# A new order of the units in the attention stage of a sparse-attention and two-layer feed-forward kernel

## The chip, the cores and the metric

The kernel runs on one NeuronCore of a Trainium2 chip. The metric is the device time of one execution in microseconds (us). The kernel before takes 877.76 us, the median of three runs (877.35 to 877.94).

## The reference

The input is an attention of 4 batches, 8 heads, 512 local and 32 global tokens, 64 numbers per head. A global token attends to all 544 tokens. A local token attends to the 32 global ones and to the local ones at most 32 positions away. The softmax takes the maximum off first and divides by the sum. What comes out, 2176 tokens of 512 numbers, goes through two feed-forward layers:

```
s_g   = scale * q_g @ k_all.T;   out_g = softmax(s_g) @ v_all
s_l   = scale * q_l @ [k_g, k_l].T, masked to |i - j| <= 32 among local keys
out_l = softmax(s_l) @ [v_g, v_l]
h = relu(x @ w1_in);  x = (h * h) @ w1_out                    # 512 -> 2048 -> 512
h = x @ w2_in;  g = P(h) / (Q(h) + 1e-6);  out = g @ w2_out   # P cubic, Q quadratic in |h|
```

All weights come as 64-bit floats. The first layer's and the second layer's weights are 16 chunks each of w_in and w_out, every one 128 x 512.

## The kernel before, in words

**Stages.** The attention stage is a loop over steps `p`. Step p = 0 to 15 belongs to one pair of heads (two heads of 64 numbers lie on the 128 partitions). Behind it lies the feed-forward stage, 2 layers x 5 tiles of tokens x 16 chunks, each chunk an `mm1` (12 matmuls into one PSUM bank) and an `mm2`. Steps 16 and 17 of the attention loop already do the first two `mm1` and their elementwise part (`ew1`).

**A unit.** A pair has two units (p, 0) and (p, 1), 256 query rows each. A unit goes through these pieces:
- S: `scores`, 8 matmuls in 64 x 64 tiles of the array (L311), into the banks `s_ps[0:2]` for unit 0 and `s_ps[2:4]` for unit 1.
- `maxima`: VectorE adds the mask and takes the row minimum of the scaled scores (L320), for each of two halves j; it also moves the scores out of PSUM. `exps`: ScalarE's exponentials with their row sums (L328).
- `sums`, `norm`: VectorE adds 1e-9 and takes the reciprocal (L332, L336), GpSimd multiplies (L339, four instructions).
- T: `transp`, five 128 x 128 transposes on TensorE into `tc_ps[0]` and `tc_ps[1]` (L357, L358). `transp_evac`: ScalarE copies the first bank out (L362), VectorE the second (L364).
- P·V: `pv`, global columns in full 128 x 128 matmuls (L382), windows in 128 x 64 tiles (L376), and for unit 1 a piece with the global queries (L396), into `pv_ps[u]`. `pv_local` and `pv_global`: VectorE copies the result into x (L403, L410, L412).
- `p_tiles` takes the buffers of the transposed probabilities; `g_copies`: GpSimd writes the global queries' probabilities into them (L350).

**The global queries.** For each group g of two pairs: G, `g_scores`, matmuls into `s_ps[0:2]` (L432; `pv_ps` for g = 0), with the maxima on VectorE (L435, L436); `g_scale` (L441); `g_exps` on ScalarE (L445, L446); `g_norm` on VectorE (L450, L451) and GpSimd (L452); Gt, `g_transp`, transposes back into `s_ps[0:2]` (L461, L462) and two ScalarE copies (L464, L465). G runs in odd steps, Gt in even ones.

**Weights.** Ten chunks of layer 1 are converted during the attention stage. `w_load` brings a chunk by DMA two steps ahead (L88), `w_scale` is ScalarE's first pass one step ahead (L94), `w_float` three VectorE passes (L106, L108, L113), `w_split` a VectorE cast (L124), `w_rest` a GpSimd subtraction (L132). `slots` says in which step a chunk is converted. `x_high` (ScalarE, L156) and `x_low` (VectorE, L161) split the first tile of x, a quarter a step, in steps 9 to 13.

**Order.** The program is inside `tc.manual_schedule()`: every engine executes its instructions in the order in which the text issues them. Waits between engines follow from the tiles that are written and read; a tile of a pool with `bufs` buffers waits until the one that lay there `bufs` allocations earlier has been read for the last time. In a step of the loop TensorE's order is now S (p, 0); T (p-1, 0); P·V (p-2, 1); G in odd steps; S (p, 1); Gt in even steps; T (p-1, 1); P·V (p-1, 0). In VectorE's queue the maxima of G stand where `g_scores` is called, and `g_scale` and `g_exps` stand ahead of the maxima and exponentials of unit (p, 1).

Of the kernel before, what the change touches and what calls it, by code (L numbers as in the profile page):

```python
# [17 lines left out]
ALU = mybir.AluOpType  # L18
# [35 lines left out]
def body(ctx, tc, qT, kW, v, w1i, w1o, w2i, w2o, coef, out):  # L54
# [209 lines left out]
    msk_p = att.enter_context(tc.tile_pool(name="msk", bufs=1))  # L264
    ident = msk_p.tile([128, 128], F32, name="ident")
    mask = msk_p.tile([128, NB, KW], F32, name="mask")
    v_p = att.enter_context(tc.tile_pool(name="v", bufs=2))
    sm_p = att.enter_context(tc.tile_pool(name="sm", bufs=4))
    pt_p = att.enter_context(tc.tile_pool(name="pt", bufs=3))
    pg_p = att.enter_context(tc.tile_pool(name="pg", bufs=2))  # L270
    st_p = att.enter_context(tc.tile_pool(name="st", bufs=4))

    ff_p = {}

# [40 lines left out]
    def maxima(p, u, j):  # L315
        s, nm = sm[p, u][:2]
        for i in range(2):
            b, k = 2 * u + i, 2 * j + i
            o = s[:, KW * i:KW * i + KW, j]
            dve.tensor_tensor_reduce(out=o, in0=s_ps[2 * u + j][:, KW * i:KW * i + KW], in1=mask[:, b],  # L320
                                     scale=-0.125, scalar=3.0e38, op0=ALU.add, op1=ALU.min,
                                     accum_out=nm[:, k:k + 1])
# [37 lines left out]
    def transp_evac(p, u):  # L360
        p1, p2 = pT[p, u]
        act.copy(bass.AP(tensor=p1.tensor, offset=p1.offset, ap=[p1.ap[0], [320, 2], [192, 2], [1, 128]]),  # L362
                 tc_ps[0].rearrange("p (a b c) -> p a b c", a=2, b=2))
        dve.tensor_copy(p2, tc_ps[1][:, 0:128])  # L364

    def pv(p, u):

        v = vt[p // 2]
        c = pgT[p // 2][1]
        p1, p2 = pT.pop((p, u))  # L370
        bank = pv_ps[u]

        def win(w, o0, o1, stop=False):
            for j in range(2):
                jj = 2 * (p % 2) + j
                pe.matmul(bank[64 * j:64 * j + 64, o0:o1], v[:, VW * w + 64 * jj:VW * w + 64 * jj + 64],  # L376
                          p1[:, j, o0 + (32 if o0 >= 128 else 0):o1 + (32 if o0 >= 128 else 0)],
                          start=False, stop=stop, skip_group_check=True)

        def glob(i):  # L380
            o = VG + 256 * (p % 2) + 128 * i
            pe.matmul(bank[:, 160 * i:160 * i + 128], v[:, o:o + 128], p2, start=i == 0, stop=False,  # L382
                      skip_group_check=True)


        glob(0)
        glob(1)
        win(4 * u, 64, 160)
        win(4 * u + 1, 0, 64)
        win(4 * u + 2, 128, 224)  # L390
        win(4 * u + 3, 224, 288, stop=u == 0)
        if u:
            for j in range(2):
                jj = 2 * (p % 2) + j
                o = VE + 64 * jj
                pe.matmul(bank[64 * j:64 * j + 64, 128:160], v[:, o:o + 64], c[:, 32 * jj:32 * jj + 32],  # L396
                          start=False, stop=True, skip_group_check=True)

    def pv_local(p, half):
        b, hp = divmod(p, 4)  # L400
# [17 lines left out]
    pg2 = [pg_p.tile([128, 128], F32, tag=f"pl{i}", name=f"pl{i}", bufs=1) for i in range(2)]  # L418

    def g_scores(g):  # L420
        c1, c2 = s_ps[:2] if g else pv_ps
        for c in (c1, c2):
            for i in range(2):
                p = 2 * g + i
                o = slice(64 * i, 64 * i + 64)
                if c is c1:
                    keys = kt[p][:, KE:KE + KW * NB].rearrange("p (a b) -> p a b", a=NB)[:, :, 0:128]
                else:
                    last = kt[p][:, KC - 64:KC]
                    keys = bass.AP(tensor=last.tensor, offset=last.offset - (KC - 64 - KE - 128),  # L430
                                   ap=[last.ap[0], [KC - 64 - KE - 128, 2], [1, 32]])
                pe.matmul(c[o] if c is c1 else c[o, 0:64], qt[p][:, SL:], keys, start=True, stop=True,  # L432
                          tile_position=(0, 64 * i))
        m = st_p.tile([128, 8], F32, tag="gm", name="gm")
        dve.tensor_reduce(m[:, 0:1], c1[:, 32:], axis=AX.X, op=ALU.max)  # L435
        dve.tensor_reduce(m[:, 1:2], c2[:, 0:64], axis=AX.X, op=ALU.max)  # L436
        pgs[g] = pg[g % 2], m, c1, c2

    def g_scale(g):
        s, m, c1, c2 = pgs[g]  # L440
        dve.tensor_scalar(m[:, 2:3], m[:, 0:1], m[:, 1:2], -0.125, op0=ALU.max, op1=ALU.mult)  # L441

    def g_exps(g):
# [25 lines left out]
    with tc.manual_schedule():  # L469
# [33 lines left out]

        early = [(0, 0, j) for j in range(N_IN0)] + [(0, 1, j) for j in range(N_OUT0)]
        slots = {}
        for p, c in zip([4, 6, 8, 10, 12, 14, 16, 16, 17, 17], early):
            slots.setdefault(p, []).append(c)

        for k in range(7):
            pe.matmul(pv_ps[0], warm[:, 0:128], warm, start=True, stop=True)  # L510
        for p in range(NP + 2):
            if p == NP:
                open_ff()
            if 1 <= p and p + 3 < NP:
                load_qk(p + 3)
            if p == 1:
                load_v(1)
            if p >= 4 and p % 2 == 0 and p // 2 < NP // 2:
                load_v(p // 2)
            for c in slots.get(p + 2, []):  # L520
                w_load(*c)
            cv = slots.get(p, [])
            cur, pre = p < NP, 1 <= p <= NP
            odd = p % 2 == 1 and p + 2 < NP
            g = (p + 1) // 2

            def step(*k):
                for c in cv:
                    w_float(*c, k)

            if cur:
                sm_tiles(p, 0)
                scores(p, 0)
                maxima(p, 0, 0)
                exps(p, 0, 0)
            else:
                mm1(p - NP)
            if 2 <= p:
                pv_local(p - 2, 0)
            if pre:  # L540
                sums(p - 1, 1)
            if cur:
                maxima(p, 0, 1)
            if pre:
                norm(p - 1, 1)
                p_tiles(p - 1, 0)
                p_tiles(p - 1, 1)
                if p > 1:
                    g_copies(p - 1, 0)
                    g_copies(p - 1, 1)  # L550
            step(0)
            if 2 <= p:
                pv_global(p - 2, 0)
            step(1)
            if pre:
                transp(p - 1, 0)
                transp_evac(p - 1, 0)
            step(2)
            if cur:
                exps(p, 0, 1)  # L560
            if 2 <= p:
                pv(p - 2, 1)
            if odd and p > 1:
                g_scores(g)
            if cur:
                sm_tiles(p, 1)
                if p == 0:
                    for k in range(4):
                        pe.matmul(pv_ps[0], warm[:, 0:128], warm, start=True, stop=True)
                scores(p, 1)  # L570
                if odd and p > 1:
                    g_scale(g)
                    g_exps(g)
                maxima(p, 1, 0)
                sums(p, 0)
                norm(p, 0)
                exps(p, 1, 0)
                maxima(p, 1, 1)
            if p == 1:
                g_transp(0)  # L580
                g_copies(0, 0)
                g_copies(0, 1)
                g_scores(g)
                g_scale(g)
                g_exps(g)
            if odd:
                g_norm(g)
            for c in cv:
                w_split(*c, dve)
                w_rest(*c)  # L590
            if p % 2 == 0 and 0 < p < NP:
                g_transp(g)
            if 2 <= p:
                pv_local(p - 2, 1)
                pv_global(p - 2, 1)
            if pre:
                transp(p - 1, 1)
                transp_evac(p - 1, 1)
            if cur:
                exps(p, 1, 1)  # L600
            if p == 0:
                for k in range(4):
                    pe.matmul(pv_ps[0], warm[:, 0:128], warm, start=True, stop=True)
                g_scores(0)
                g_scale(0)
                g_exps(0)
                g_norm(0)
            if pre:
                pv(p - 1, 0)
            for c in slots.get(p + 1, []):  # L610
                w_scale(*c)
            if 9 < p <= 9 + KD:
                x_low(0, p - 10)
            if 9 <= p < 9 + KD:
                x_high(0, p - 9)
            if p >= NP:
                ew1(p - NP)
        att.close()
        act.activation(nf[:, 0:4], cf[:, 0:4], AF.Copy, scale=-1.0)
# [24 lines left out]
        split = []  # L644
        made = []
        back = list(reversed(second))
        used = [1, -1]

        def load():

# [45 lines left out]

        load()
        magnitudes(2)
        for s in range(2, 2 * S1):
            t, j = divmod(s, KF)  # L700
            mm1(s)
            if j >= LAG:
# [99 lines left out]
```

## Time and profile before

| | us |
|---|---|
| median of three runs | 877.76 |
| the profiled execution | 878.36 |
| its span, first to last instruction | 876.6 |
| PE busy in the span | 866.3 |
| VectorE (DVE) busy | 614.2 |
| ScalarE (ACT) busy | 548.2 |
| GpSimd (POOL) busy | 249.7 |

The granted TensorE clock was 1.0 of full speed over the whole span. PE is TensorE's matmuls, whose ends are modelled: they overlap in the pipeline, so the time that one needs is the distance from its start to the next start, and a busy PE row hides short waits. DVE and ACT instructions overlap a little in the same way. A row "x4" stands for four merged instructions and gives the start of the first and the time that they cover. In the chain of waits each row is a stretch in which that instruction was what the end of the program waited for.

### The profile page before, as it was taken

What the parts mean: (1) busy time and instruction counts of PE and PEld (TensorE: products, weight loads), DVE (VectorE), ACT (ScalarE), POOL (GpSimd) and SP (SyncE); (2) the same over time, 40 slices, a digit from 0 to 9 for tenths busy, and PEclk for the clock granted to TensorE, in tenths of its full rate; (3) what the DMA queues carried; (4) which work ended last, traced back from release to release, by engine and by line L of the source; (5) the groups of instructions that cost most, each with busy time, mean ns of one, the idle gap of its engine ahead of it and who ended that gap; (6) DMA issues with size and microseconds to landing.
All of it is one profiled execution on the core that took longest, in us unless ns stands there. A gap on an engine that the chain in (4) does not pass through costs nothing.

```text
span 876.6 us, 14522 instructions
## 1 busy us (share of the span) xinstructions
PE 866.3 (99%) x5335; PEld 772.1 (88%) x5335; DVE 614.2 (70%) x1355; ACT 548.2 (63%) x1173; POOL 249.7 (28%) x326
## 2 busy tenths in 40 slices
PE   8999999999999999999999999999999999999998
PEld 4777788888888999999999978888888999999998
DVE  5788888855554576552422599769777987987986
ACT  6888857763332343432444588668666876886885
POOL 4787854420000000000156342212221221221221
PEclk9999999999999999999999999999999999999999
DMA  9787549101653176140034200010001001001001
GB/s 348 273 329 264 222 151 409 41 1 37 178 142 113 39 220 190 54 147 1 15 119 125 73 20 1 0 49 1 1 0 49 1 1 37 1 1 37 1 1 37
DMA packets 27574, 81.67 MB, mean 93 GB/s; under 512 B 3184, under 2 KB 4976, under 8 KB 26480
## 3 DMA queue, kind: packets, MB, share of 16 engines
q1 hardware_dynamic: 27504, 80.76, 27.0%
q8 instruction: 42, 0.69, 0.3%
q14 instruction: 28, 0.23, 0.1%
HBM read 67.90 MB, written 12.85 MB: 92 GB/s over the span
## 4 chain that ended last, share of the span: by engine, by line
PE 92%; DVE 3%; POOL 2%; ACT 1%; issue 1%; DMA 1%; SPq 0%; POOLq 0%; ACTq 0%
PE tc L188 21%; PE pv L188 21%; PE s L175 14%; PE s L177 14%; PE s L176 14%; POOL sm L339 2%; PE pv L376 2%; PE tc L357 2%; PE pv L382 1%; PE s L311 1%; DMA k<-in_kW_dram 1%; DVE sm L320 1%; PE s L432 1%; DVE tt L251 0%; ACT gs L445 0%
## 5 line engine op out<-in xcount | busy, mean ns | idle before, releaser
L175 PE MATMUL s<-xh,w 128*128 128x384 f32 (+1 forms) x640 | 229.7, 359 | 0.0
L177 PE MATMUL s<-xh,w 128*128 128x384 f32 (+1 forms) x640 | 228.4, 357 | 0.0
L176 PE MATMUL s<-xl,w 128*128 128x384 f32 (+1 forms) x640 | 228.3, 357 | 0.0
L260 POOL TENSOR_TENSOR gl<-tt,gh 128x384 fp32r<-128x384 f32 (+1 forms) x79 | 89.8, 1137 | 268.2 <-ACT gh L259 205.2
L188 PE MATMUL tc<-gh,w 128*128 128x384 f32 (+1 forms) x640 | 152.8, 360 | 0.8 <-ACT gh L259 0.8
L188 PE MATMUL pv<-gh,w 128*128 128x384 f32 (+1 forms) x640 | 152.5, 360 | 0.0
L217 ACT ACTIVATE a<-s 128x384 f32<-128x384 f32 (+1 forms) x80 | 42.5, 531 | 156.1 <-PE s L177 156.1
L177 PEld LDWEIGHTS s<-xh,w 128*128 128x128 f32 x640 | 120.1, 188 | 11.4
L176 PEld LDWEIGHTS s<-xl,w 128*128 128x128 f32 x640 | 120.2, 188 | 10.8
L175 PEld LDWEIGHTS s<-xh,w 128*128 128x128 f32 x640 | 120.1, 188 | 10.5
L188 PEld LDWEIGHTS tc<-gh,w 128*128 128x128 f32 x640 | 115.9, 188 | 12.5 <-ACT gh L259 1.7
L188 PEld LDWEIGHTS pv<-gh,w 128*128 128x128 f32 x640 | 115.9, 188 | 11.8
L132 POOL TENSOR_TENSOR w<-raw,w 128x512 fp32r<-128x512 f32 x32 | 42.5, 1346 | 278.8 <-ACT w L126 265.5
L223 DVE TENSOR_TENSOR b<-a 128x384 f32<-128x384 f32 (+1 forms) x64 | 38.4, 599 | 116.1 <-ACT a L217 116.1
L188 PE MATMUL pv<-gl,w 128*128 128x384 f32 (+1 forms) x320 | 89.4, 360 | 0.0
L188 PE MATMUL tc<-gl,w 128*128 128x384 f32 (+1 forms) x320 | 89.2, 359 | 0.0
L237 DVE SCALAR_TENSOR_TENSOR a<-a,nf,b 128x384 f32<-128x384 f32 (+1 forms) x80 | 53.4, 667 | 32.3 <-ACT b L235 32.2
L234 ACT ACTIVATE a<-s 128x384 f32<-128x384 f32 (+1 forms) x80 | 42.0, 525 | 52.9 <-PE s L177 52.9
L339 POOL TENSOR_SCALAR sm<-sm,rs 128x160 f32<-128x160 f32 x128 | 59.1, 486 | 27.7 <-DVE x L410 8.7
L250 DVE SCALAR_TENSOR_TENSOR a<-a,b 128x384 f32<-128x384 f32 (+1 forms) x80 | 49.0, 612 | 22.0 <-ACT b L245 22.0
L188 PEld LDWEIGHTS tc<-gl,w 128*128 128x128 f32 x320 | 58.7, 188 | 6.0
L188 PEld LDWEIGHTS pv<-gl,w 128*128 128x128 f32 x320 | 58.7, 188 | 5.8
(117 smaller groups left out, 1344.8 us busy)
## 6 DMA issues: line engine op xcount, KB each, us to landing
v<-in_v_dram SPq DMA_DIRECT2D x8, 1408.0 KB, 8.3
k<-in_kW_dram SPq DMA_DIRECT2D x15, 592.0 KB, 6.5
r<-in_w1i_dram SPq DMA_DIRECT2D x16, 512.0 KB, 9.6
r<-in_w1o_dram SPq DMA_DIRECT2D x16, 512.0 KB, 10.2
raw<-in_w2i_dram SPq DMA_DIRECT2D x16, 512.0 KB, 4.1
st<-cv SPq DMA_DIRECT2D x32, 256.0 KB, 4.3
raw<-in_w2o_dram SPq DMA_DIRECT2D x16, 512.0 KB, 4.0
raw<-st SPq DMA_DIRECT2D x32, 256.0 KB, 2.7
```

The source lines that it names most:

```text
L132: pool.tensor_tensor(w[:, 1], f, w[:, 0].bitcast(F32), op=ALU.subtract)
L175: pe.matmul(ph, wh, hi[:, kk, :n], start=(kk == 0), stop=False)
L176: pe.matmul(ph, wh, lo[:, kk, :n], start=False, stop=False)
L177: pe.matmul(ph, wl, hi[:, kk, :n], start=False, stop=(kk == KD - 1))
L188: pe.matmul(acc_bank[d][:, :n], w[:, half, 128 * d:128 * d + 128], src[:, :n], start=start, stop=stop)
L217: act.activation(a, ph, AF.Relu)
L223: dve.tensor_tensor(b, a, a, op=ALU.mult)
L234: act.activation(a, ph, AF.Square)
L237: dve.scalar_tensor_tensor(a, in0=a, scalar=nf[:, 5:6], in1=b, op0=ALU.mult, op1=ALU.add)
L250: dve.scalar_tensor_tensor(a, in0=a, scalar=EPS1, in1=b, op0=ALU.add, op1=ALU.mult)
L260: eng.tensor_tensor(gl, t, gh.bitcast(F32), op=ALU.subtract)
L339: pool.tensor_scalar(e, e, rs[:, k:k + 1], 1.0, op0=ALU.mult, op1=ALU.mult)
```

## The change

The loop gets one step more (16 to 18 beside the pairs), and the third `mm1` moves into it. In a step, TensorE's order becomes S (p, 0); T (p-1, 0); P·V of (p-3, 1) with the global columns first; G in odd steps; P·V of (p-2, 0) with the global columns last; Gt in even steps; T (p-2, 1); S (p, 1). A unit (p, 1) is therefore scored at the end of step p, has its maxima and exponentials at the start of step p+1, is transposed at the end of step p+2 and multiplied with V in step p+3. The maxima of G move from `g_scores` to `g_scale`, which together with `g_exps` stands behind the sums of unit (p, 0). G of the second group goes to the transposes' banks. The VectorE part of `transp_evac` becomes a function of its own. Buffers: v 3 instead of 2, sm 6 instead of 4, pt 5 instead of 3, st 6 instead of 4. The slots of the ten early chunks move from steps 4, 6, 8, 10, 12, 14, 16, 16, 17, 17 to 8, 10, 12, 14, 16, 16, 17, 17, 18, 18, and a chunk of a step up to 14 is converted in two parts: two `w_float` passes at the end of its step, the third, the cast and the subtraction at the end of the next. The diff's core:

```diff
-    v_p = att.enter_context(tc.tile_pool(name="v", bufs=2))
-    sm_p = att.enter_context(tc.tile_pool(name="sm", bufs=4))
-    pt_p = att.enter_context(tc.tile_pool(name="pt", bufs=3))
+    v_p = att.enter_context(tc.tile_pool(name="v", bufs=3))
+    sm_p = att.enter_context(tc.tile_pool(name="sm", bufs=6))
+    pt_p = att.enter_context(tc.tile_pool(name="pt", bufs=5))
...
-        dve.tensor_copy(p2, tc_ps[1][:, 0:128])
+
+    def transp_evac2(p, u):
+        dve.tensor_copy(pT[p, u][1], tc_ps[1][:, 0:128])
...
-        glob(0)
-        glob(1)
-        win(4 * u, 64, 160)
+        if u:
+            glob(0, start=True)
+            glob(1)
+        win(4 * u, 64, 160, start=not u)
         win(4 * u + 1, 0, 64)
         win(4 * u + 2, 128, 224)
-        win(4 * u + 3, 224, 288, stop=u == 0)
+        win(4 * u + 3, 224, 288)
...
+        else:
+            glob(0)
+            glob(1, stop=True)
...
-        c1, c2 = s_ps[:2] if g else pv_ps
+        c1, c2 = s_ps[:2] if g > 1 else tc_ps if g else pv_ps
...
-        for p, c in zip([4, 6, 8, 10, 12, 14, 16, 16, 17, 17], early):
+        for p, c in zip([8, 10, 12, 14, 16, 16, 17, 17, 18, 18], early):
...
-        for p in range(NP + 2):
+        for p in range(NP + 3):
...
+            a = (p - 1, 0) if pre else None
+            b = (p - 3, 1) if 3 <= p else None
+            c = (p - 2, 0) if 2 <= p <= NP + 1 else None
+            d = (p - 2, 1) if 2 <= p <= NP + 1 else None
+            odd, even = p % 2 == 1 and 1 < p < NP - 2, p % 2 == 0 and 0 < p < NP
...
             if cur:
                 sm_tiles(p, 0)
                 scores(p, 0)
+            elif p - NP < 3:
+                mm1(p - NP)
+            if pre and p > 2:
+                maxima(p - 1, 1, 0)
+                exps(p - 1, 1, 0)
+            if cur:
                 maxima(p, 0, 0)
                 exps(p, 0, 0)
+            for n in (a, d):
+                if n:
+                    p_tiles(*n)
+                    if p > 1:
+                        g_copies(*n)
+            if a:
+                transp(*a)
+                transp_evac(*a)
+            if cur:
+                maxima(p, 0, 1)
+                exps(p, 0, 1)
+            if pre and p > 2:
+                maxima(p - 1, 1, 1)
+                exps(p - 1, 1, 1)
+            if a:
+                transp_evac2(*a)
+            if b:
+                pv(*b)
+            if odd:
+                g_scores(g)
+            if c:
+                pv(*c)
+            if b:
+                pv_local(*b)
+                pv_global(*b)
+            if even:
+                g_transp(g)
+            if d:
+                transp(*d)
+            if cur:
+                sums(p, 0)
+                norm(p, 0)
+            if odd:
+                g_scale(g)
+                g_exps(g)
             if pre:
                 sums(p - 1, 1)
+                norm(p - 1, 1)
+            if c:
+                pv_local(*c)
+                pv_global(*c)
+            if d:
+                transp_evac(*d)
+                transp_evac2(*d)
+            if odd:
+                g_norm(g)
+            for w in first:
+                w_float(*w, (0, 1))
+            for w in second:
+                w_float(*w, (2,))
+            for w in whole:
+                w_float(*w)
+            for w in second + whole:
+                w_split(*w, dve)
+                w_rest(*w)
             if cur:
                 sm_tiles(p, 1)
...
                 scores(p, 1)
+            if p < 2:
+                for j in range(2):
+                    maxima(p, 1, j)
+                    exps(p, 1, j)
...
+            if p == 1:
+                g_transp(0)
+                g_copies(*a)
+                g_scores(1)
+                g_scale(1)
+                g_exps(1)
+                g_norm(1)
...
-        for s in range(2, 2 * S1):
+        for s in range(3, 2 * S1):
```

## Rows read from the trace of the kernel before

**Rows 1.** The page, the chain that ended last, share of the span by engine

```profile
PE 92%; DVE 3%; POOL 2%; ACT 1%; issue 1%; DMA 1%; SPq 0%; POOLq 0%; ACTq 0%
```

**Rows 2.** Windows: stretch, length, busy of PE, PEld, DVE, ACT, POOL, clock, DMA

```profile
24.95:57.64 32.69, 32.06 (x468) 25.43 (x465) 26.18 (x151) 27.28 (x107) 23.36 (x54) 1.00 0.72 265
57.64:110.89 53.25, 51.52 (x737) 40.94 (x733) 46.88 (x247) 47.04 (x178) 42.76 (x90) 1.00 0.68 262
...
80.56:94.13 13.57, 13.12 (x187) 10.32 (x185) 12.57 (x65) 12.13 (x46) 11.03 (x22) 1.00 0.57 219
```

**Rows 3.** The chain of waits in 54.06:67.22: start, us, what

```profile
54.06 0.94 PE s L432 x4
...
55.02 0.66 DVE gm L435
...
57.00 0.69 POOL sm L339 x2
```

**Rows 4.** Timeline of TensorE, one unit, and T behind Gt: start, us, instruction

```profile
64.41 0.77 PE L311 MATMUL s<-k,q 64*64 64x160 f32 x16
65.12 0.74 PE L357 MATMUL tc<-ident,sm 128*128 128x128 f32 x4
...
66.35 0.78 PE L376 MATMUL pv<-p,v 128*64 128x96 f32 x16
...
67.05 0.63 PE L432 MATMUL s<-k,q 128*64 128x512 f32 x2
...
23.11 0.64 PE L357 MATMUL tc<-ident,sm 128*128 128x128 f32 x4
...
24.23 0.78 PE L376 MATMUL pv<-p,v 128*64 128x96 f32 x16
```

**Rows 5.** Timeline of ScalarE: an evacuation and half a unit's exponentials

```profile
71.11 0.58 ACT L362 COPY p<-tc 128x512 f32<-128x512 f32 x1
71.57 0.46 ACT L328 ACTIVATE sm<-sm,nm 128x160 f32<-128x160 f32 x1
...
72.44 0.68 ACT L94 ACTIVATE cv<-r 128x512 f32<-128x512 f32 x1
```

**Rows 6.** Timeline of VectorE in 71.9:75.3

```profile
72.65 0.32 DVE L320 CUSTOM_DVE_ANT_0 sm<-s,mask 128x160 f32<-128x160 f32 x1
...
73.23 0.40 DVE L106 TENSOR_SCALAR cv<-cv 128x512 int32<-128x512 int32 x1
...
73.66 0.78 DVE L108 SCALAR_TENSOR_TENSOR cv<-r,cv 128x512 int32<-128x512 int32 x1
74.37 0.28 DVE L364 COPY p<-tc 128x128 f32<-128x128 f32 x1
74.57 0.69 DVE L113 SCALAR_TENSOR_TENSOR cv<-r,cv 128x512 int32<-128x512 int32 x1
```

**Rows 7.** Groups by line in 22:104: shapes and count, busy us, mean ns, idle before

```profile
L403 DVE COPY x<-pv 128x256 f32<-128x256 f32 x24 | 9.9, 413 | 0.0
...
L124 DVE CAST w<-cv 128x512 fp32r<-128x512 f32 x6 | 3.1, 522 | 0.0
L161 DVE TENSOR_TENSOR xl<-x,xh 128x512 fp32r<-128x512 f32 x4 | 3.1, 782 | 0.0
```

**Rows 8.** Timeline in 0:14: VectorE's first maxima of pair 1

```profile
13.29 0.31 DVE L320 CUSTOM_DVE_ANT_0 sm<-s,mask 128x160 f32<-128x160 f32 x1
```

**Rows 9.** The chain of waits in 110:126: end of mm1(0), start of mm1(3)

```profile
113.85 0.47 PE tc L357 x4
...
124.77 0.23 PE s L175
```

**Rows 10.** Timeline: sums alone, and sums beside a GpSimd instruction

```profile
72.57 0.17 DVE L332 TENSOR_SCALAR rs<-sum 128x4 f32<-128x4 f32 x1
...
78.72 1.27 POOL L132 TENSOR_TENSOR w<-cv,w 128x512 fp32r<-128x512 f32 x1
79.33 0.70 DVE L332 TENSOR_SCALAR rs<-sum 128x4 f32<-128x4 f32 x1
```

More of the change, by code (lines that the diff above doesn't have):

```diff
@@ L266, in body @@
     mask = msk_p.tile([128, NB, KW], F32, name="mask")
-    v_p = att.enter_context(tc.tile_pool(name="v", bufs=2))
-    sm_p = att.enter_context(tc.tile_pool(name="sm", bufs=4))
-    pt_p = att.enter_context(tc.tile_pool(name="pt", bufs=3))
+    v_p = att.enter_context(tc.tile_pool(name="v", bufs=3))
+    sm_p = att.enter_context(tc.tile_pool(name="sm", bufs=6))
+    pt_p = att.enter_context(tc.tile_pool(name="pt", bufs=5))
     pg_p = att.enter_context(tc.tile_pool(name="pg", bufs=2))
-    st_p = att.enter_context(tc.tile_pool(name="st", bufs=4))
+    st_p = att.enter_context(tc.tile_pool(name="st", bufs=6))
     ff_p = {}
@@ L369, in pv, with win @@
         c = pgT[p // 2][1]
-        p1, p2 = pT.pop((p, u))
+        p1, p2 = pT.pop((p, u))[:2]
         bank = pv_ps[u]
-        def win(w, o0, o1, stop=False):
+        def win(w, o0, o1, start=False):
             for j in range(2):
@@ L377, in win, with glob @@
                           p1[:, j, o0 + (32 if o0 >= 128 else 0):o1 + (32 if o0 >= 128 else 0)],
-                          start=False, stop=stop, skip_group_check=True)
-        def glob(i):
+                          start=start, stop=False, skip_group_check=True)
+        def glob(i, start=False, stop=False):
             o = VG + 256 * (p % 2) + 128 * i
-            pe.matmul(bank[:, 160 * i:160 * i + 128], v[:, o:o + 128], p2, start=i == 0, stop=False,
+            pe.matmul(bank[:, 160 * i:160 * i + 128], v[:, o:o + 128], p2, start=start, stop=stop,
                       skip_group_check=True)
-        glob(0)
-        glob(1)
-        win(4 * u, 64, 160)
+        if u:
+            glob(0, start=True)
+            glob(1)
+        win(4 * u, 64, 160, start=not u)
         win(4 * u + 1, 0, 64)
         win(4 * u + 2, 128, 224)
-        win(4 * u + 3, 224, 288, stop=u == 0)
+        win(4 * u + 3, 224, 288)
         if u:
@@ L434, in g_scores @@
         m = st_p.tile([128, 8], F32, tag="gm", name="gm")
-        dve.tensor_reduce(m[:, 0:1], c1[:, 32:], axis=AX.X, op=ALU.max)
-        dve.tensor_reduce(m[:, 1:2], c2[:, 0:64], axis=AX.X, op=ALU.max)
         pgs[g] = pg[g % 2], m, c1, c2
@@ L440, in g_scale @@
         s, m, c1, c2 = pgs[g]
+        dve.tensor_reduce(m[:, 0:1], c1[:, 32:], axis=AX.X, op=ALU.max)
+        dve.tensor_reduce(m[:, 1:2], c2[:, 0:64], axis=AX.X, op=ALU.max)
         dve.tensor_scalar(m[:, 2:3], m[:, 0:1], m[:, 1:2], -0.125, op0=ALU.max, op1=ALU.mult)
@@ L523, in body @@
             cur, pre = p < NP, 1 <= p <= NP
-            odd = p % 2 == 1 and p + 2 < NP
+            a = (p - 1, 0) if pre else None
[3 more added lines that the diff above has]
+            odd, even = p % 2 == 1 and 1 < p < NP - 2, p % 2 == 0 and 0 < p < NP
             g = (p + 1) // 2
-            def step(*k):
-                for c in cv:
-                    w_float(*c, k)
+            first = cv if p < NP else []
+            whole = cv if p >= NP else []
+            second = slots.get(p - 1, []) if p <= NP else []
             if cur:
@@ L533, in body @@
                 scores(p, 0)
+            elif p - NP < 3:
[4 more added lines that the diff above has]
+            if cur:
                 maxima(p, 0, 0)
                 exps(p, 0, 0)
[L536 to L539, printed above, removed]
+            for n in (a, d):
[3 more added lines that the diff above has]
+                        g_copies(*n)
@@ L540, in body @@
+            if even:
[8 more added lines that the diff above has]
+                g_exps(g)
             if pre:
                 sums(p - 1, 1)
-            if cur:
-                maxima(p, 0, 1)
-            if pre:
                 norm(p - 1, 1)
[L546 to L564, printed above, removed]
+            if c:
[4 more added lines that the diff above has]
+                transp_evac2(*d)
@@ L570, in body @@
                 scores(p, 1)
[L571 to L600, printed above, removed]
+            if p < 2:
+                for j in range(2):
+                    maxima(p, 1, j)
+                    exps(p, 1, j)
             if p == 0:
@@ L607, in body @@
                 g_norm(0)
[L608 to L611, printed above, removed]
+            if p == 1:
[5 more added lines that the diff above has]
+                g_norm(1)
+            for w in slots.get(p + 1, []):
+                w_scale(*w)
             if 9 < p <= 9 + KD:
@@ L615, in body @@
                 x_high(0, p - 9)
-            if p >= NP:
+            if NP <= p:
                 ew1(p - NP)
@@ L646, in body @@
         back = list(reversed(second))
-        used = [1, -1]
+        used = [2, -1]
         def load():
```

## The prediction

> **What bounds the kernel now.** Read the chain of waits on the page first: TensorE has 92% of it [rows 1], so the time is TensorE's own work plus what it waits for. Then the windows by stage [rows 2]. From 110.89 us on, the first feed-forward matmuls lie between the last attention units and TensorE does not stop; nothing of that work is altered. So the time moves with the moment at which the fourth chunk of the feed-forward part, `mm1(3)`, starts: 124.77 us now [rows 9]. Whatever the change does it does before that.
>
> In the attention part a step is one pair of heads, two units. Two steps take 13.1 to 13.6 us (13.57 in [rows 2]). Next the chain inside one such stretch [rows 3]: the global scores (G) end at 55.00, VectorE takes maxima from 55.02, ScalarE the exponentials, and only then, 1.98 us later, may GpSimd start the normalisations of a local unit (57.00), on which its transposes wait. The global softmax stands in line ahead of the local one. The timeline of a unit without such a wait [rows 4] gives what TensorE itself needs: S 0.71 (64.41 to 65.12), T and the global columns of P·V 1.23, the windows with their global piece 0.70: 2.64. Two steps are 4 x 2.64, plus G 0.94 [rows 3], plus the transposes of the global rows (Gt), five like T's, some 0.6: 12.1. TensorE thus loses 1.0 to 1.5 us in every two steps. The other engines are nearly full too: in the stretch of 13.57, VectorE is busy 12.57 and ScalarE 12.13 [rows 2].
>
> **The change, part by part.**
>
> *TensorE's order.* Each unit now changes the array's tile shape three times (S to T, global columns to windows, windows to S or T), six changes in a step; S T G W, W G T S has four, since S meets S and W meets W. What does a change cost? T with its global columns takes 1.23 after S and 1.12 after Gt's full-width transposes [rows 4], so at least 0.11; the upper bound is 0.23, which would leave S only 0.48 of its 0.71. I take 0.16, nearer to the row that shows one directly. That is 0.32 a step: TensorE's own two steps become 11.45.
>
> *The waits.* The first unit's transposes come a step later than its scores, as now, and the second's late in the step after that. Two buffers of probabilities and two of statistics more, and two of transposed ones, cover that. The local normalisations no longer stand behind the global chain, so the 1.98 us go. Late next is the one consumer that stays: S of the following pair overwrites the two banks that hold the global scores, so it waits for the global exponentials.
>
> *VectorE, by spacing.* A half unit's two maxima take 0.49 (0.32 each, of which 0.08 overlaps the next: L108 is 0.78 long and the next starts 0.71 later); L106, L108 and L113 0.31, 0.71 and 0.61; the small evacuation 0.20 [rows 6]; L403 0.33, the cast 0.43, `x_low` 0.70, lengths less the same overlap [rows 7]. Sums with their reciprocal I take at 0.30, x's global piece at 0.10, the global maxima at 1.0, `g_norm` at 0.33: together with the eight groups above they come to 10.9 for two steps with one chunk converted, what VectorE is busy in windows like [rows 2]. *ScalarE*: a half unit's exponentials 0.87, an evacuation 0.46 [rows 5], the global exponentials 0.94 (the rest of the 1.98).
>
> Now one step on VectorE, from its first instruction (0.00) in the new order. Four maxima groups to 1.96, evacuation and x of the older unit to 2.59. The sums of the first unit need ScalarE: it starts at 0.37, does two groups of exponentials, an evacuation and a third group by 3.45. So VectorE waits from 2.59 to 3.55, is through with sums at 3.85, in an even step waits again for the fourth group until 4.4, then sums 0.30, x 0.43, evacuation 0.20: 5.3. An odd step has the global maxima in place of the second wait and `g_norm` behind the exponentials: 6.15. Behind that stand the conversion pieces: L106 and L108 (1.02) in an even step, L113 and the cast (1.05) in an odd one, and 0.70 for `x_low` in steps 10 to 13. None of it lies in the waits, for the queue is in order. So VectorE's two steps are 11.45 without conversion, 13.55 with, 14.95 with `x_low`. Once VectorE is behind, TensorE is held twice a step: G waits for maxima of the banks it overwrites, S for the global exponentials (5.85 behind VectorE's start) or for the copies after Gt (4.9).
>
> *The conversions.* Those of steps 4 and 6 go to 16 to 18, beside the first feed-forward matmuls. There VectorE has 4.1 us of conversion in each of three steps, so it ends step 18 some 5 us later than TensorE; the first chunk that this could hold up is used four mm1/mm2 rounds on, so I cost it at nothing. Its DMA waits for the attention buffers, freed at about 121; also hidden. If that cover were gone, each late chunk would cost up to the 2.05 of one conversion.
>
> **The sum.**
> - *Start, to step 4.* Unchanged to 13.29, VectorE's first maxima of pair 1 [rows 8]. Now the second group's scores sit in the transposes' banks, so T of unit (1,0) waits for: maxima 0.98, evacuation 0.2, exponentials and sums (16.5), maxima of (1,1) 17.5, global maxima 18.5, ScalarE's copies 19.3, global exponentials 20.3. Then T 0.7, P·V 1.15, Gt 0.6, T 0.7, S 0.7, with handovers: step 3 starts at 24.4. Now it starts at 24.95 [rows 2], but with one T and two P·V (3.0 us) done more. Step 3 waits for its normalisation; step 4 starts at 30.5.
> - *Steps 4 to 7*, no conversion: TensorE 11.45, VectorE 11.45, with handovers 11.7 for two: 53.9. (Now: step 8 starts at 57.64, with the 3.0 us done more.)
> - *Steps 8 to 15.* VectorE: 6.35 + 7.2 + 7.05 + 7.9 + 7.05 + 7.9 to the start of step 14, 43.45; S of step 15 follows 4.9 later, and the step's TensorE work without G is 4.95: 53.3. So `mm1(0)` starts at 107.2. Now the same steps take 53.25 [rows 2]: nothing is gained there.
> - *The tail.* `mm1(0)` takes 2.96 (110.89 to 113.85 [rows 2, 9]), later ones 2.78 where no shape changes. Of [rows 4] less T 0.6, P·V is 1.21 with the global piece, 1.15 without. Step 16: 2.96 + T 0.6 + 1.21 + 1.15 + T 0.6; step 17: 2.78 + 1.21 + 1.15 + 0.6; step 18: 2.78 + 1.21 and a change 0.2. Sum 16.45: `mm1(3)` at 123.65.
>
> 123.65 against 124.77: 1.1 us earlier. The profiled execution took 878.36 (span 876.6 and 1.76 around it) and would take 877.25; it lies 0.6 above the median of the runs, 877.76, so the forecast is 876.7. A measurement of this kernel tells 0.2%, about 1.75 us, from no change. This is inside it: below 876.0 I call faster, above 879.5 slower.
>
> **A rule that speaks against it.** A VectorE `TENSOR_SCALAR` that started at 79.33 lasted 0.70, to the moment when GpSimd's L132 (78.72, 1.27 long) ended; the same instruction's usual length is about 0.17 [rows 10]. The Trainium skill, "SBUF — State Buffer", section "Who interferes with whom", says that VectorE's second pair of ports is GpSimd's, and that whoever issues first holds it for the whole instruction while the other fully blocks. The row agrees with that. What it would do here is the second rival below.
>
> **Rivals.**
> 1. *VectorE's work does overlap, and TensorE is fed.* If the waits that I see at 2.59 and 3.85 fill themselves, because conversions end while TensorE is still at the previous step's last units, steps 8 to 15 go by VectorE's busy time: 11.9, 12.57, 12.57, 10.9 for two steps each, 47.9 instead of 53.3. 871.3. For it: [rows 2] shows VectorE at 93% of a stretch, so such density is reached now, and the deeper buffers. Against it: the order inside a step is fixed, and ScalarE starts each step on VectorE's first maxima.
> 2. *GpSimd's normalisations block VectorE* (slower). The second sums of a step are issued just behind the first unit's normalisation, and L106 and the cast behind the second's. One normalisation is about 0.39 (0.69 for not quite two in [rows 3]). Where the `TENSOR_SCALAR` always finds one running it waits 0.2 on average, twice a step, and VectorE's step grows by 0.35 over 12 steps: 4.2 us, 880.9. It decides from a mean of 0.15 a step upward, since 1.1 us in all then goes back to no gain and more. For it: the row at 79.33. Against it: beside a GpSimd that is idle the same instruction keeps its 0.17, and where TensorE sets the pace VectorE has slack.
> 3. *A shape change costs nothing in the new order.* Then steps 4 to 7 lose the 0.65 for two steps and the tail about 1.0: 879.0, still no change. It lies in the forecast's own range.
>
> **How the numbers follow.** The forecast, VectorE's serial step, has 0.42; its own range is 874.5 to 879 (half a microsecond for the start, 0.1 to 0.3 a step for handovers, the bounds of the shape change); of it 0.12 lies below 876.0 and 0.02 above 879.5. Rival 1 has 0.32, nearly all faster. Rival 2 has 0.26: 0.20 slower, 0.06 within. Faster 0.43, same 0.35, slower 0.22. The range that leaves no more than two in ten out: 870.5 to 881.
>
> **What would show it.** Right: steps 4 to 7 at 5.7 to 6.0 us each and steps 10 to 13 at 7 or more; VectorE waiting for ScalarE's L328 ahead of the sums, ScalarE for VectorE's maxima at each step's start; TensorE waiting for the global exponentials (L445, L446) ahead of S in odd steps; `mm1(3)` near 123.7 and no TensorE wait behind it. The shape changes: S behind S without the 0.2 gap of today. Wrong: steps 8 to 15 as short as 4 to 7 (rival 1); `TENSOR_SCALAR` of VectorE at 0.3 or more on average (rival 2); a TensorE wait for a converted weight after 124 us, which I cost at nothing; or step 3 starting later than 25.

## The result, and the profile after

The changed kernel takes 883.86 us (median of 4 runs, 881.63 to 884.30) beside 877.84 for the kernel before on the same chip: ratio 1.0062 [1.005, 1.0074], slower by 6.0 us. The forecast was 876.7 in a range of 870.5 to 881.0. The profiled execution took 884.25, with a span of 882.5.

The page's line on the chain of waits, to be held against [rows 1]:

```profile
PE 81%; DVE 2%; ACT 1%; issue 0%; DVEq 0%
```

The chain is followed back only to 138.57 us, so it says nothing of the attention part. To find the place, take one event that both kernels have in every step, the start of S for the second unit (L311), and cut both spans there:

| stretch | before | after | difference |
|---|---|---|---|
| start to S(3,1) | 28.68 | 31.86 | +3.18 |
| S(3,1) to S(7,1), steps 4 to 7 | 26.31 | 24.02 | -2.29 |
| S(7,1) to S(15,1), steps 8 to 15 | 52.69 | 56.51 | +3.82 |
| S(15,1) to the first mm2 | 19.65 | 20.01 | +0.36 |
| the next four feed-forward rounds, each an `mm2` and an `mm1` | 22.24 | 22.93 | +0.69 |
| the rest of the span | 727.00 | 727.14 | +0.14 |

Steps 4 to 7 gain, but they also lost the two conversions that they had before. The change loses at the start, in the steps with conversions, and a little in the feed-forward part. The same cuts as windows of the kernel after (stretch, length, busy of PE, PEld (TensorE's weight loads), DVE, ACT, POOL, granted clock, DMA), to be held against [rows 2]; the fourth is two steps alone, as the third of [rows 2]:

```profile
24.95:31.86 6.91, 6.91 (x98) 5.39 (x96) 4.76 (x28) 4.95 (x20) 3.10 (x10) 0.91 0.38 133
31.86:55.88 24.02, 24.02 (x372) 20.25 (x371) 18.53 (x115) 21.19 (x85) 15.52 (x43) 1.00 0.78 293
55.88:112.39 56.51, 50.34 (x733) 41.16 (x733) 45.54 (x240) 45.73 (x173) 40.48 (x85) 1.00 0.69 268
...
82.86:98.20 15.34, 13.12 (x186) 10.46 (x185) 12.59 (x64) 12.21 (x46) 11.37 (x23) 1.00 0.89 352
```

In steps 4 to 7 TensorE is busy all of 24.02. In steps 8 to 15 every engine is idle for 6 us or more, so none is busy all the time: they wait for each other. And in the first line the clock is below 1.00.

**The start.** The timeline of the kernel after around step 2 (start, us, instruction, idle before and what ended it):

```profile
17.07 0.65 DVE L445 TENSOR_REDUCE gm<-tc 128x1 f32<-128x480 f32 x1
...
18.77 0.66 ACT L451 ACTIVATE gs<-tc,gm 128x480 f32<-128x480 f32 x1
...
19.66 1.10 PE L357 MATMUL tc<-ident,sm 128*128 128x128 f32 x4 [2.97 <-ACT gs L451]
...
23.19 1.06 PE L467 MATMUL s<-ident,gs 128*128 128x128 f32 x4
```

T of unit (1,0) needs the banks that hold the second group's global scores, so it waits for their maxima (L445) and exponentials (L451): TensorE stands still for 2.97 us. Then its instructions are long: the four matmuls of Gt at 23.19 take 1.06, the same four two steps later 0.60:

```profile
36.52 0.60 PE L467 MATMUL s<-ident,gs 128*128 128x128 f32 x4
```

The windows of the same stretch tell why (the clock is the third number from the end):

```profile
17.50:20.00 2.50, 0.34 (x2) 0.37 (x3) 0.72 (x4) 2.31 (x10) 1.88 (x6) 0.87 1.04 423
20.00:22.50 2.50, 2.50 (x22) 2.05 (x21) 1.39 (x11) 1.98 (x8) 1.19 (x3) 0.50 0.99 404
22.50:25.00 2.50, 2.50 (x13) 2.46 (x13) 1.06 (x6) 1.01 (x4) 1.62 (x5) 0.50 0.44 176
25.00:27.50 2.50, 2.50 (x39) 1.90 (x38) 1.08 (x6) 1.14 (x5) 1.90 (x6) 0.76 0.00 0
```

After the wait the granted clock is at 0.50, the lower of its two levels (1.2 instead of 2.4 GHz). The kernel before has 1.00 in all four windows, and no wait on TensorE above 0.48 us between 15 and 30 us.

**Steps 8 to 15.** VectorE in one even step, step 12, which begins for it at 86.84, and what hangs on it:

```profile
86.84 0.31 DVE L320 CUSTOM_DVE_ANT_0 sm<-s,mask 128x160 f32<-128x160 f32 x1
...
90.39 0.17 DVE L332 TENSOR_SCALAR rs<-sum 128x4 f32<-128x4 f32 x1 [0.89 <-ACT sm L328]
...
91.23 0.17 DVE L332 TENSOR_SCALAR rs<-sum 128x4 f32<-128x4 f32 x1 [0.47 <-ACT sm L328]
...
91.72 0.92 PE L311 MATMUL s<-k,q 64*64 64x160 f32 x16 [0.62 <-ACT pg L470]
...
92.14 0.63 DVE L106 TENSOR_SCALAR cv<-cv 128x512 int32<-128x512 int32 x1
...
92.81 0.79 DVE L108 SCALAR_TENSOR_TENSOR cv<-r,cv 128x512 int32<-128x512 int32 x1
...
93.52 0.68 DVE L161 TENSOR_TENSOR xl<-x,xh 128x512 fp32r<-128x512 f32 x1
...
94.12 0.31 DVE L320 CUSTOM_DVE_ANT_0 sm<-s,mask 128x160 f32<-128x160 f32 x1
...
94.47 0.45 ACT L328 ACTIVATE sm<-sm,nm 128x160 f32<-128x160 f32 x1 [1.63 <-DVE nm L320]
...
95.23 1.20 PE L438 MATMUL s<-k,q 128*64 128x512 f32 x7 [0.55 <-DVE nm L320]
```

VectorE stands idle ahead of both sums (L332), 0.89 and 0.47, because ScalarE's exponentials are not done. Behind the sums in its queue stand L106, L108 and `x_low` (L161), 2.0 us of work that waits for nothing from ScalarE in this step. While VectorE does them ScalarE is idle, 1.63 us, for the next step's maxima. Each waits for the other in turn, and TensorE waits for both (91.72, 95.23). Summed over the eight steps (engine, line, waited for: us, times, longest):

```profile
ACT sm L328 <- DVE nm L320: 9.0, 7, 1.6
DVE rs L332 <- ACT sm L328: 8.6, 12, 0.9
PEld s L311 <- ACT gs L451: 3.4, 3, 1.2
PEld s L311 <- ACT pg L470: 2.6, 3, 0.9
...
PEld s L438 <- DVE nm L320: 2.0, 5, 0.7
```

**The feed-forward part.** The first matmul of the first chunk, `mm1(0)`, and of the fourth, `mm1(3)`, and the waits of TensorE's weight loads in 112 to 200 us:

```profile
113.09 0.50 PE L175 MATMUL s<-xh,w 128*128 128x512 f32 x1
...
129.53 0.50 PE L175 MATMUL s<-xh,w 128*128 128x512 f32 x1
```

```profile
PEld s L175 <- ACT a L217: 2.5, 10, 0.7
PEld tc L188 <- POOL w L132: 0.4, 1, 0.4
```

The kernel before has no such wait from 110 us on. L217 is ScalarE's evacuation of an `mm1`. The chain shows why one of them is late: from 140.27 to 146.32 us it runs over weight conversions of VectorE and ScalarE. ScalarE is idle for 5.39 us ahead of a cast (L126, at 142.49) that waits for VectorE's last pass (L113), and L217 stands behind that cast in its queue.

### The profile page after: what moved, and what is told of

It is laid out like the page before. It is cut to its first block, busy times and chain, and to the rows that moved or that the text cites. A ratio compares the mean times of both kernels' runs of the same rounds, so it can differ in the third digit from the quotient of the medians.

```text
span 882.5 us, 14488 instructions
## 1 busy us (share of the span) xinstructions
PE 866.3 (98%) x5335; PEld 773.5 (88%) x5335; DVE 619.4 (70%) x1355; ACT 548.8 (62%) x1173; POOL 247.6 (28%) x326
## 4 chain that ended last, share of the span: by engine, by line
PE 81%; DVE 2%; ACT 1%; issue 0%; DVEq 0%
PE tc L188 21%; PE pv L188 21%; PE s L175 13%; PE s L177 13%; PE s L176 13%; DVE tt L251 0%; DVE tt L252 0%; DVE gl L225 0%; DVE a L237 0%; ACT b L245 0%; ACT b L244 0%; DVE s L108 0%; DVE a L250 0%; DVE s L106 0%; ACT s L94 0%
## 5 line engine op out<-in xcount | busy, mean ns | idle before, releaser
L217 ACT ACTIVATE a<-s 128x384 f32<-128x384 f32 (+1 forms) x80 | 42.5, 531 | 152.7 <-PE s L177 152.7
L132 POOL TENSOR_TENSOR w<-raw,w 128x512 fp32r<-128x512 f32 x32 | 42.5, 1345 | 271.0 <-ACT w L126 249.0
L339 POOL TENSOR_SCALAR sm<-sm,rs 128x160 f32<-128x160 f32 x128 | 56.8, 472 | 38.5 <-ACT sm L328 28.9
L328 ACT ACTIVATE sm<-sm,nm 128x160 f32<-128x160 f32 x128 | 55.2, 440 | 19.8 <-DVE nm L320 19.8
```

Source lines behind the costliest of these rows:

```text
L132: pool.tensor_tensor(w[:, 1], f, w[:, 0].bitcast(F32), op=ALU.subtract)
L217: act.activation(a, ph, AF.Relu)
L328: act.activation(e, e, AF.Exp, scale=-1.0, bias=nm[:, k:k + 1], accum_out=tot[:, k:k + 1])
L339: pool.tensor_scalar(e, e, rs[:, k:k + 1], 1.0, op0=ALU.mult, op1=ALU.mult)
```

## The experiments

Four theories. A: the clock falls because of the 2.97 us wait at the start. B: in steps 8 to 15 the order of VectorE's queue costs the time, not the amount of its work. C: the later slots of the conversions free steps 4 to 7 and cost something in the feed-forward part. D: a change of TensorE's tile shape costs time, and the new order saves two of them a step. Ratios are to the kernel before, run beside each (878.02 and 878.11).

**e1_warm** fills the wait of TensorE with ten matmuls that nobody reads.

```diff
                 scores(p, 0)
+                if p == 2:
+                    for k in range(10):
+                        pe.matmul(s_ps[3], warm[:, 0:128], warm, start=True, stop=True)
```

> The changed kernel with ten filler matmuls in TensorE's wait of 2.97 us at the start of step 2 (into a bank that is free there); nothing else. Theory A, the clock: the granted clock fell to half (0.50 in 20:25) because TensorE stood still from 16.7 to 19.7; with the filler it stays at 1.00, T to S of step 2 takes 4.7 us instead of 6.7, and the whole is 2 to 3 us shorter: about 881 us, with the same gap and the same steps behind it. Rival, the wait itself costs and the clock nothing: T of unit (1,0) still starts at 19.7, so 883.9 with no change.

Measured 881.90, ratio 1.0044 [1.003, 1.0057], 2.0 below the change. In its timeline and one of its windows, TensorE works through the wait and keeps its clock:

```profile
17.42 2.32 PE L548 MATMUL s<-raw 128*128 128x512 bf16 x10 [0.52 <-DVE nm L320]
...
19.88 0.72 PE L357 MATMUL tc<-ident,sm 128*128 128x128 f32 x4
```

```profile
20.00:22.50 2.50, 2.50 (x31) 2.27 (x32) 1.55 (x11) 1.79 (x8) 1.19 (x3) 1.00 0.92 375
```

T starts 0.2 us later than without the filler (19.88, 19.66), yet S(3,1) starts 2.18 earlier (29.68). From T to S(3,1) it is 9.80 instead of 12.20. So it is the clock and not the wait itself: A holds.

**e2_fill** gives VectorE the conversion while it waits for ScalarE. Same instructions, other places in its queue: the cast goes ahead of `g_norm`, and `x_low` of even steps between the two sums.

```diff
...
+            for w in first:
+                w_float(*w, (0, 1))
+            for w in second:
+                w_float(*w, (2,))
             if cur:
                 sums(p, 0)
...
+            for w in second:
+                w_split(*w, dve)
+                w_rest(*w)
             if odd:
                 g_norm(g)
-            for w in first:
-                w_float(*w, (0, 1))
-            for w in second:
-                w_float(*w, (2,))
...
```

> The changed kernel with the same VectorE work in another place of the same step: the first two conversion passes, or the third, in VectorE's wait ahead of the sums of unit (p,0) (0.9 us in each step), the cast ahead of g_norm, x_low of steps 10 and 12 in the second wait. Theory B, in-order waits: VectorE's two steps shrink from 14.8 to 15.3 us to about 12.7, the three pairs of steps from 68.1 to 112.4 us from 44.3 to some 38, the whole by 5 to 7 us: 877 to 879. Rival, VectorE is at its throughput (12.6 busy of 15.3 with its handovers) or is blocked by GpSimd: under 1 us.

Measured 875.88, ratio 0.9972 [0.9961, 0.9984]: 8.0 below the change, more than expected, and a little faster than the kernel before. Between the two profiled executions it is 8.2: 7.6 in steps 8 to 15, and 0.7 at the start, where this run too has the wait of 2.97 us but keeps the lower clock for a shorter time (0.59 and 0.72 in the windows that had 0.50):

```profile
20.00:22.50 2.50, 2.14 (x17) 1.84 (x19) 1.55 (x11) 1.79 (x9) 1.27 (x4) 0.59 0.96 384
22.50:25.00 2.50, 2.50 (x22) 2.33 (x18) 1.02 (x6) 1.47 (x6) 0.93 (x3) 0.72 0.58 232
```

Next its windows for steps 8 to 15 and for two steps of them, then the two waits that had been 9.0 and 8.6:

```profile
55.19:104.14 48.95, 48.70 (x734) 40.38 (x733) 45.74 (x242) 46.04 (x175) 37.62 (x86) 1.00 0.80 311
...
79.77:92.50 12.73, 12.64 (x187) 10.28 (x186) 12.25 (x65) 12.14 (x46) 10.78 (x23) 1.00 0.87 328
```

```profile
ACT sm L328 <- DVE nm L320: 1.1, 3, 0.4
...
DVE rs L332 <- ACT sm L328: 0.5, 2, 0.3
```

48.95 instead of 56.51, with VectorE busy for as long (45.74, 45.54). TensorE is now busy for all but 0.25. B holds.

**e3_noconv** leaves out VectorE's passes that turn the raw weights to floats (L106, L108, L113) for the four chunks of steps 8 to 15.

```diff
-            for w in first:
-                w_float(*w, (0, 1))
             for w in second:
-                w_float(*w, (2,))
+                del raws[w]
```

> The changed kernel without the three VectorE float passes of the four chunks converted in steps 8 to 15 (1.63 us each, 6.5 us in all; the weights of those chunks are then wrong); the cast, the subtraction and all DMAs stay. Theory B: the steps without x_low go at TensorE's pace of 6.0 us, those with it at 6.5 or so; the stretch 55.9 to 112.4 us shortens from 56.5 to about 50, 877 to 878 in all. Rival, ScalarE or the global exponentials set the pace: under 2 us shorter.

Measured 877.77, ratio 0.9999 [0.999, 1.0008]; steps 8 to 15 take 50.79. That is longer than in e2_fill, which does all the passes while TensorE is busy almost throughout. Here the cast (L124) and `x_low` (L161) still stand at the end of the queue; which of the two costs the difference was not tested. The work in the right place beats leaving these passes out.

**e4_slots** puts the conversions back into the steps that they had before.

```diff
-        for p, c in zip([8, 10, 12, 14, 16, 16, 17, 17, 18, 18], early):
+        for p, c in zip([4, 6, 8, 10, 12, 14, 16, 16, 17, 17], early):
```

> The changed kernel with the ten chunks in their old steps 4, 6, 8, 10, 12, 14, 16, 16, 17, 17. Theory C, VectorE's backlog of step 18 is what delays the first feed-forward rounds by about 1.2 us: these go, while steps 4 to 7 grow from 6.0 to 6.8 us each (3 us): 885 to 886 in all. Rival, steps 4 to 7 have room for two chunks: 882.5.

Measured 886.79, ratio 1.0097 [1.0083, 1.0111]. Steps 4 to 7 take 26.19 (+2.17 on the change), steps 8 and 9 14.15 (+1.95), and the four feed-forward rounds 22.21: the 0.7 is gone, and so are the waits of its weight loads for L217 and L132. (At the start the profiled execution happens to be 1.75 faster than the change's, with the lower clock for a shorter time, as in e2_fill.) C holds: the later slots cost 0.7 there, and save more only as long as the conversions stand in the wrong place. And with the same two conversions the kernel before needed 26.31 for steps 4 to 7: the new order alone gains 0.1 there as it stands.

**e5_both** is e1_warm and e2_fill together; **e6_slots** is that with the slots of e4_slots.

> The edits of e1_warm and e2_fill together. Theories A and B are of different stretches, so their gains add: 883.9 less 2.0 less 8.0, 873.5 to 874.5. Rival: with the steps no longer held by VectorE the earlier start is lost again in a wait behind it: 876.

> e5_both with the ten chunks in their old steps 4 to 17. Theory C with B: with the conversion in VectorE's waits a chunk in steps 4 to 7 costs nothing (12.0 us for two steps as in steps 8 and 9 of e2_fill), and the 0.7 us of the first feed-forward rounds (22.9 instead of 22.2 us for the first two) go: 0.5 to 1 us below e5_both. Rival: steps 4 to 7 grow as they did in e4_slots, by 1.1 us for two: 1.5 us above it.

Measured 874.27, ratio 0.9955 [0.9942, 0.9969], and 873.45, ratio 0.9948 [0.9934, 0.9961]. In e5_both the two gains add up. In e6_slots steps 4 to 7 take 23.80, as in e5_both: two conversions more, beside TensorE, at no cost. The four feed-forward rounds (the expectation counts them as two) take 22.24, as in the kernel before. e6_slots has the lowest median, 4.7 us below the kernel before.

**e7_start** is e2_fill with those slots and, in place of the filler, the second group's global scores and exponentials (and the first group's Gt, which stands ahead of them) ahead of unit (1,1)'s maxima.

```diff
...
+            if p == 1:
+                g_transp(0)
+                g_copies(*a)
+                g_scores(1)
+                g_scale(1)
+                g_exps(1)
             if p < 2:
                 for j in range(2):
                     maxima(p, 1, j)
...
```

> e2_fill with the old steps of the chunks, and without filler: in step 1 the second group's scores, maxima and exponentials go ahead of the maxima and exponentials of unit (1,1), so that the transposes' banks come free earlier. Theory A: T of unit (1,0) starts at about 18.1 instead of 19.7, TensorE's wait is 1.4 us instead of 3, too short for the clock to fall (1.00 throughout, as before the change with a wait of 1.3 us), and the whole is at or up to 1 us below e6_slots: 872 to 873. Rival: the clock falls with any wait there: 2 us above e6_slots.

Measured 873.84, ratio 0.9954 [0.9941, 0.9966]: the same as e6_slots within the intervals, with no dummy work. T comes 1.4 us earlier than in the change, and the clock stays up in the profiled execution:

```profile
18.25 0.71 PE L357 MATMUL tc<-ident,sm 128*128 128x128 f32 x4 [1.43 <-ACT gs L451]
```

```profile
20.00:22.50 2.50, 2.50 (x34) 2.08 (x32) 0.18 (x2) 2.50 (x12) 0.68 (x3) 1.00 0.95 381
```

**e8_shapes** is e7_start with the global columns first in both units, so that TensorE changes its shape six times a step and not four.

```diff
...
-        if u:
-            glob(0, start=True)
-            glob(1)
-        win(4 * u, 64, 160, start=not u)
+        glob(0, start=True)
+        glob(1)
+        win(4 * u, 64, 160)
...
```

> e7_start with the global columns first in both units, as before the change, so that the array's tile shape changes six times in a step again and not four; all else as e7_start. Theory D, a change costs 0.16 us: 0.32 a step where TensorE sets the pace, 12 to 16 steps, 3 to 5 us above e7_start. Rival, a change is hidden or nothing: the same time within 0.5 us.

Measured 875.16, ratio 0.9967 [0.9955, 0.9979], 1.3 above e7_start where more was expected. From T of a step to S of the next, on TensorE: first e7_start, then e8_shapes.

```profile
42.66 0.74 PE L357 MATMUL tc<-ident,sm 128*128 128x128 f32 x4
...
47.06 1.32 PE L311 MATMUL s<-k,q 64*64 64x160 f32 x32
48.31 0.74 PE L357 MATMUL tc<-ident,sm 128*128 128x128 f32 x4
...
53.13 1.10 PE L311 MATMUL s<-k,q 64*64 64x160 f32 x20
```

```profile
43.01 0.74 PE L357 MATMUL tc<-ident,sm 128*128 128x128 f32 x4
...
47.68 1.32 PE L311 MATMUL s<-k,q 64*64 64x160 f32 x32
48.93 0.74 PE L357 MATMUL tc<-ident,sm 128*128 128x128 f32 x4
...
54.10 1.18 PE L311 MATMUL s<-k,q 64*64 64x160 f32 x28
```

4.40 becomes 4.67 and 4.82 becomes 5.17, with two changes more in each: 0.14 to 0.18 for one. Steps 4 to 7 take 24.68 instead of 23.77, steps 8 and 9 12.34 instead of 12.06, less than the changes alone would make: S at the end of odd steps takes 1.59 in e7_start (41.07 to the next T) and 1.25 here, for a reason that stays open. Steps 10 to 15, where TensorE has waits to spare, take the same (36.89 and 36.85), and from `mm1(0)` to the first `mm2` it is 0.7 more. So the whole costs only 1.3. D holds in its mechanism, and less was at stake than the expectation had.

## Why the prediction was wrong

By its own terms, for the profiled execution: it would have been 877.25 and was 884.25, 7.0 more.

- *The start*: step 4 was to start at 30.5. S(3,1) starts at 31.86, and step 4 half of a 1.25 us pair of S later, at 32.5: +2.0. The wait itself was foreseen, even too long (T at 20.3, seen at 19.66). The step that failed is that T, P·V and Gt behind it were costed at full speed. TensorE runs them at half its clock, so that step 3 starts at 26.39 and not at 24.4; the prediction had named a start after 25 as a sign of being wrong. In e1_warm, where the clock stays up, step 3 starts at 23.72 and step 4 at 30.28, so the rest of this sum was about right. The prediction did not ask what the wait would do to the clock. How long the clock stays down differs from execution to execution: in e2_fill and e4_slots, with the same wait, it cost 1.0 from T to S(3,1) and not 2.4. So the size of this term is in part chance. Even the fastest run of the change, 881.63, lies above the range.
- *Steps 4 to 7*: 23.4 forecast, 24.0 seen, +0.6. TensorE sets the pace, as said. In e7_start two of its steps with both S at 1.25 would be 11.72 (from T at 42.66 to 53.13, and 1.25), 0.27 over the forecast 11.45, and S of odd steps shows a further third of a microsecond (1.59 from 41.07 to T), where 0.25 was put for handovers. The price of a shape change, 0.16, was right. The stretch gained 2.29, but only together with the conversions' moving out (e4_slots).
- *Steps 8 to 15*: 53.3 forecast, 56.6 from 32.5 + 24.0 to `mm1(0)` at 113.09: +3.3, the largest term. The mechanism was the one forecast, almost to the hundredth: in step 12 the first sums come 3.55 after VectorE's start (3.55 forecast), the second 4.39 (4.4), L106 5.30 (5.3). Behind that L106 takes 0.67 to the next instruction instead of 0.31, for two reasons. The 0.31 was read where another instruction followed:

```profile
73.54 0.18 DVE L410 COPY x<-pv 128x32 f32<-128x32 f32 x1
```

In the new order L108 follows, which reads what L106 writes; in steps 4 to 15 of both kernels it starts 0.03 to 0.04 after L106's end. With L106 at 0.40 that is 0.12 more. The other 0.24 is that L106 itself takes longer (below). Over steps 8, 10 and 12 the two make 1.1. VectorE's six steps from 8 to 13 take 45.07 (57.12 to 102.19) instead of 43.45: 1.6. The handover from TensorE's step to VectorE's at step 8 adds 0.6 (56.5 to 57.12). Step 15, costed as TensorE's work alone, takes 6.03 from S at 107.06 instead of 4.95, with a wait of 0.39 for ScalarE's evacuation in it: 1.1.
- *The tail*: 16.45 forecast, 129.53 - 113.09 = 16.44.
- *The feed-forward part*, "hidden": +1.1. Of it 0.69 and 0.14 are in the rows of the first table. TensorE's loads wait for the evacuation of `mm1` (L217) and once for a converted weight (L132), the wait that the prediction named as what would show it wrong; e4_slots shows that the later slots of the conversions cause it. The other 0.3 is at `mm1(3)`: it now stands behind a shape change, and 124.77 [rows 9] is not the start of its first matmul, which lies at 124.61.

2.0 + 0.6 + 3.3 + 1.1 = 7.0. So the mechanism in the largest part was right and its size wrong: the prediction saw that the conversions could not overlap in VectorE's order, and put their stretch at no change, where it lost 3.8. And two terms were put at nothing that were not: the clock behind the wait, and the late conversions.

**The rivals.** The first, that VectorE's work overlaps, had 47.9 for steps 8 to 15: not in this order, but e2_fill, with the queue written so that it can, takes 48.95. The second, GpSimd's normalisations blocking VectorE's sums, did not come true where it was priced: in steps 8 to 15 the sums take 0.16 to 0.17 each, less than the mean of before (0.24), though GpSimd normalises beside half of them. What did grow is L106: 0.63 to 0.66 in all four cases, each issued while L339 runs, and 0.40 before [rows 6]. In e2_fill none of the four has L339 beside it: three take 0.42, and the fourth, beside GpSimd's `g_copies` (L350), 0.75. The Trainium skill's "SBUF — State Buffer", "Who interferes with whom", has the rule that where VectorE and GpSimd contend for the shared ports, the one that issues first holds them for the whole instruction and the other waits. The trace agrees for L106 here and not for the sums, which L339 does not hold up. At 0.24 three times L106's growth is 0.7 of the 3.3, and no run tested it alone. The third, that shape changes are free, is refuted by e8_shapes. The Trainium skill's "TensorEngine Tiling (Array Packing)", "Key Properties", says that a change of tiling mode drains the engine, without a price; the trace agrees that a change costs time, 0.14 to 0.18 us each here.

## What to carry to other kernels

In an in-order queue, work that needs nobody belongs ahead of the instruction that waits, not behind it: the same instructions in other places were worth 7.6 us of 56.5 here, more than leaving three of the passes out. When a change puts a wait of about 3 us on TensorE, cost what follows it at half the clock too, or fill the wait. Read an instruction's spacing where its successor is the one that it will have. Where every engine is idle for a tenth of a stretch, as here, look for two engines that each wait for the other.

## What was not expected of the hardware

A wait of 2.97 us put TensorE's granted clock at 0.50, in the change's profiled execution throughout 20 to 25 us and beyond. S(3,1) came 2.2 later than with the filler; in e2_fill and e4_slots the same wait cost less. A wait of 1.43 us (e7_start) left the clock up in the profiled execution; two other runs of e7_start, at a mean clock of 0.998, took up to 1.7 us longer than its median. The spread of the changed kernel's runs goes with it: mean clock 0.996 with spans of 882.5, 0.998 with 881.7, 0.999 with 879.8. e1_warm, at 0.999 to 1.000, spreads over 0.9 us only. And VectorE's int32 `TENSOR_SCALAR` (L106) grew from 0.40 to 0.64 beside GpSimd's normalisations, while the small one of the sums, issued beside the same work, kept its 0.17.
